# The last of four transposed tiles goes from DMA to TensorE, and a hand-written order is laid out anew

## The chip, the core and the metric

The kernel runs on one core of one Trainium2 chip. The metric is the device time of one execution in microseconds. The kernel before takes 169.82 us, the median of three runs (169.5 to 170.22).

## What is computed

The reference is one pre-norm transformer block on a 2048 x 512 activation in bf16: linear attention with 32 heads of width 16, then a dense layer with relu. Cut to what matters:

```python
x = A_x                                   # 1 x 2048 x 512
n = layernorm(x)                          # over the last axis, eps 1e-5, no gain or bias
q, k, v = heads(n @ wqkv)                 # 32 heads of 16
pq, pk = phi(q), phi(k)                   # phi(t) = where(t > 0, t + 1, exp(t)) + 1e-6
kv = einsum("bhsd,bhse->bhde", pk, v);  z = sum over s of pk
o = einsum("bhqd,bhde->bhqe", pq, kv) / (einsum("bhqd,bhd->bhq", pq, z) + 1e-6)
h = x + o.reshape(B, S, D) @ wo
out = h + relu(layernorm(h) @ w1) @ w2    # w1 512 x 1792, w2 1792 x 512
```

## The kernel before

Every instruction's place is written by hand. `ORDER` (line 18) is a string of words such as `x.2` or `p.0.11.7`; the loop at the end (line 564) takes them one by one and calls `op_x(2)`, `op_p(0, 11, 7)` and so on. Each engine, and each engine's DMA queue, works through its own instructions in the order of the words. The numbers in a word are the tile or block, the piece, and for words of TensorE the PSUM bank (of eight) that takes the result. An operation waits until its inputs are there and until the bank or buffer that it writes has been read.

The 2048 rows are 16 tiles of 128, and four blocks of four tiles. The work runs through these stages:

- First norm: `lx` loads x on SP's queue, `S` and `A` take statistics on VectorE (lines 254, 255), `R` makes the reciprocal deviation on ScalarE (260, 261), `N` normalises on VectorE (268). The normalised tile is transposed into `lnT` either by TensorE (`T`, line 293, four 128 x 128 transposes against the identity) with a copy out of PSUM by ScalarE (`E`, line 303), or by a DMA transpose on SP's queue (`X`, line 314).
- Keys and state: `K` (322) are the key projections, `F`, `U`, `M`, `D` (340, 343, 347, 350) apply phi, `G` (374) collects the state. `za` to `zh` add up the keys, `z` (398) reduces them on TensorE.
- Queries: `Q` (330) projects, `qF`, `qU`, `qM`, `qD` apply phi, again at lines 340 to 350. `d4` (446), `dl4` and `dx4` (452, 457) make one over the denominator of a block. `wb` (474) writes it to a scratch in DRAM, and eight `rb` or `ab` (477) read it back, spread over the partitions, into `rr`. `dm` (493) multiplies the queries of a block with `rr`, in two halves; it needs all eight loads.
- `kv`, `kx`, `m`, `mA`, `mD` (420 to 438) join the state with `wv` and `wo` into one 512 x 512 matrix.
- `h` (502) multiplies and `hD` (508) adds x: tile t of the attention's result.
- Second norm: `s` and `a` (256, 257) take the statistics of h, `n` on VectorE (276) or `nA` on ScalarE (282) subtracts the mean into `hn`; `x` (315) transposes `hn` into `lnT` by DMA on SP's queue. All 16 tiles go this way, `x.0` to `x.3` for block 0. The deviation is applied at the very end.
- First FFN matmul: `p` (517) makes one of 14 pieces of a block from `w1` and all four tiles of `lnT`. For four pieces of block 0 it is split: `ph` (526) takes two tiles at a time, half 0 (tiles 0 and 1) and half 1 (tiles 2 and 3). `pD` on VectorE (537), once `pA` on ScalarE (532), applies relu to two pieces at once.
- Second FFN matmul: `f` (546) multiplies with `w2`, 14 matmuls a tile, mostly in two groups of seven. `fo` (554) scales and adds h, `fd` (561) stores. The last tile is cut by columns.

The words that the change adds use two functions that stand in the kernel and that the old order does not call:

```python
def op_t(t, b):
    at_bank["t", t, 0] = transpose(hn[:, t % NQ, :], b, 0, KD)

def op_v(t):
    nc.vector.tensor_copy(out=lnT_of(t), in_=at_bank["t", t, 0])

op_x = lambda t: nc.sync.dma_start_transpose(out=lnT_of(t), in_=hn[:, t % NQ, :])
```

`transpose` (line 290) issues four 128 x 128 transposes into one bank as bf16; the copy moves 128 x 512 bf16 from that bank to `lnT`.

Of the kernel before, what the change touches and what calls it, by code (L numbers as in the profile page):

```python
# [15 lines left out]


ORDER = """
table const lx.0.1 warm.66.7.64 lx.1.1 masks lx.2.1 lk.0.4 lx.3.1 S.0 lx.4.2 S.1 lx.6.2 lq.0.4 A.0 A.1 S.2 R.0.1
warm.2.7 lx.8.4 R.1.1 N.0 lx.12.4 A.2 N.1 T.0.1 R.2.1 T.1.5 E.0 N.2 E.1 T.2.2 S.3 K.0.0 E.2 A.3 S.4 K.2.2.2.2  # L20
R.3.1 K.2.2.0.2 F.0.1 N.3 S.5 U.0.1 T.3.3 K.1.6.0.2 E.3 A.4 A.5 K.1.6.2.2 S.7 R.4.2 K.3.1.0.2 M.0.1 F.1.1 S.6
K.3.1.2.2 U.1.1 Q.0.1.5 N.4 F.2.1 A.6 N.5 A.7 F.3.1 T.4.6 M.1.1 X.5 D.0.1 Q.0.0.4 R.6.2 D.1.1 M.2.1 U.3.1 M.3.1
Q.0.2.0 N.7 lo.0.2 E.4 S.9 X.7 U.2.1 Q.0.3.1 N.6 qU.0.0.2 D.3.1 K.4.2 S.15 X.6 qF.0.0.2 S.8 K.5.3 D.2.1 qM.0.0.2
qF.0.2.2 G.3 A.8 A.9 S.12 R.8.2 G.0 S.14 F.4.2 N.9 G.2 A.12 N.8 X.9 U.4.2 S.13 G.1 A.15 A.14 A.13 qD.0.0.2 X.8
R.12.2 K.6.2 qU.0.2.2 M.4.2 S.11 K.7.3 lv.0.2 R.14.2 N.12 N.13 X.12 K.9.1 S.10 F.6.2 D.4.2 K.8.0 U.6.2 lv.2.2 A.10
M.6.2 X.13 G.4 N.14 U.8.2 N.15 D.6.2 G.5 X.15 F.8.2 za.4.1 G.6 A.11 X.14 M.8.2 K.12.0 R.10.2 qM.0.2.2 N.10 K.13.1
N.11 X.10 D.8.2 G.7 za.6.0 F.12.2 X.11 K.14.2 U.12.2 qD.0.2.2 K.15.3 M.12.2 l1.2.2 za.8.0 l2.0.7 K.10.0 F.14.2
D.12.2 K.11.1 U.14.2 zf G.9 M.14.2 F.10.2 D.14.2 G.8 U.10.2 zhi M.10.2 G.12 zlo D.10.2 G.14 z.1.0 z.2.0 z.3.0
z.0.0 G.15 zc zh d4.0.3 G.11 dl4.0 dx4.0 G.10 wb.0 G.13 lo.2.2 Q.1.0.1 gA.2.2 gD.0.2 rb.0.6 Q.1.1.2 ab.0.3 rb.0.2
ab.0.7 rb.0.4 kv.0.0 kv.2.0 ab.0.1 rb.0.0 kv.1.0 kv.3.0 ab.0.5 l1.0.2 Q.1.3.6 kx qF.1.0.2 Q.1.2.5 qU.1.0.2  # L30
qM.1.0.2 m.0.3 m.1.4 Q.2.3.7 qF.1.2.2 mD.0.2 Q.2.1.1 qU.1.2.2 qM.1.2.2 dm.0.0.2 m.2.3 m.3.4 Q.2.0.0 dm.0.2.2
mA.2.2 qD.1.0.2 h.1.6 qU.2.0.2 qD.1.2.2 h.0.2 hD.1 qF.2.0.2 h.3.3 s.1 hD.0 Q.2.2.6 a.1 s.0 nA.1 d4.1.2 a.0 h.2.1
hD.3 x.1 nA.0 s.3 qF.2.2.2 Q.3.0.5 x.0 a.3 hD.2 dl4.1 Q.3.3.4 n.3 qU.2.2.2 s.2 x.3 Q.3.2.3 a.2 dx4.1 n.2 Q.3.1.6
qM.2.0.2 qF.3.2.2 x.2 qM.2.2.2 ph.0.2.0.0 qU.3.2.2 qM.3.2.2 ph.0.3.1.0 wb.1 ph.0.0.2.0 qF.3.0.2 qD.3.2.2
ph.0.1.3.0 qD.2.2.2 ph.0.1.3.1 qU.3.0.2 ph.0.0.2.1 qM.3.0.2 rb.1.6 p.0.11.7 rb.1.3 pD.0.0.2 rb.1.1 ph.0.3.1.1
rb.1.0 p.0.10.6 qD.2.0.2 rb.1.7 qD.3.0.2 rb.1.4 p.0.9.2 rb.1.2 pD.0.10.2 rb.1.5 p.0.6.5 l2.7.7 d4.2.6.2 ph.0.2.0.1
dl4.2 p.0.5.4 r.0.4 dm.1.0.2 dl4.3 p.0.4.3 dx4.2 dm.1.2.2 h.4.7 pD.0.2.2 wb.2 pA.0.4.2 p.0.7.6 dx4.3 hD.4 p.0.8.1
pD.0.6.2 h.5.7 pD.0.8.2 rb.2.4 p.0.13.4 rb.2.7 rb.2.3 hD.5 h.6.5 rb.2.0 rb.2.6 f.1.2.0.7 hD.6 rb.2.5 s.5 rb.2.2
rb.2.1 p.0.12.3 wb.3 h.7.1 pD.0.12.2 f.0.7.7.7 hD.7 s.4 f.2.4.0.7 s.7 a.5 a.4 dm.2.0.2 f.1.2.7.7 n.4 dm.2.2.2 a.7
n.5 rb.3.2 s.6 rb.3.6 h.9.0 rb.3.3 h.8.1 x.4 hD.9 a.6 f.0.7.0.7 n.7 r.4.4 fo.1 x.7 n.6 s.9 f.3.5.0.7 rb.3.1 x.6  # L40
h.10.0 x.5 h.11.3 f.3.5.7.7 f.2.4.7.7 fo.3 hD.8 fd.3 rb.3.7 p.1.13.2 fo.2 rb.3.4 fd.1 hD.11 p.1.12.1 rb.3.5 a.9
fo.0 fd.2 p.1.2.6 rb.3.0 hD.10 p.1.3.7 pD.1.12.2 p.1.6.0 pD.1.2.2 p.1.0.3 dm.3.0.2 p.1.7.1 dm.3.2.2 h.13.7
pD.1.6.2 p.1.1.4 hD.13 p.1.4.5 pD.1.0.2 p.1.5.6 s.13 p.1.9.3 pD.1.4.2 h.12.7 p.1.8.2 hD.12 s.10 p.1.11.5 s.8
p.1.10.4 pD.1.8.2 h.14.1 s.11 h.15.7 hD.14 a.10 f.7.0.0.7 a.11 n.9 hD.15 n.11 pD.1.10.2 f.6.7.0.7 a.8 n.10 r.8.4
s.14 x.10 f.4.1.0.7 n.8 x.8 f.5.5.0.7 x.9 f.5.5.7.7 x.11 f.4.1.7.7 fo.5 fd.0 s.12 a.13 f.7.0.7.7 a.12 fo.4 a.14
f.6.7.7.7 fo.7 n.14 n.12 s.15 p.2.10.5 fo.6 p.2.11.6 n.13 fd.6 a.15 n.15 r.12.4 x.12 p.2.13.1 p.2.12.0 fd.5 x.13
p.2.9.4 pD.2.12.2 p.2.8.3 x.15 p.2.2.1 pD.2.8.2 x.14 p.2.3.2 pD.2.10.2 p.2.0.3 fd.7 pD.2.2.2 p.2.1.4 p.2.7.6
pD.2.0.2 p.2.6.5 p.3.8.1 pD.2.6.2 p.3.9.2 p.3.12.3 pD.3.8.2 p.3.13.4 p.3.2.0 pD.3.12.2 p.2.4.6 p.3.10.5 p.3.6.1
p.2.5.7 p.3.4.3 pD.2.4.2 p.3.5.4 p.3.7.2 f.11.7.0.7 pD.3.6.2 pD.3.4.2 f.11.7.7.7 p.3.3.1 f.10.3.7.7 pD.3.2.2
p.3.11.6 p.3.0.4 pD.3.10.2 f.8.1.0.7 f.10.3.0.7 p.3.1.5 f.8.1.7.7 pD.3.0.2 fo.10 f.15.0.0.14.3.1 f.15.6.0.14.0.2  # L50
fo.15.3.1 fd.15.3.1 f.13.4.0.7 fo.15.0.2 fd.15.0.2 fd.4 f.13.4.7.7 f.14.5.7.7 fo.13 fo.11 fd.13 fd.10 f.12.6.0.7
fo.8 fd.8 fd.11 f.14.5.0.7 f.9.7.0.7 f.9.7.7.7 f.12.6.7.7 fo.9 fo.14 fd.9 f.15.3.0.14.2.1 fd.14 fo.12 fd.12
fo.15.2.1 fd.15.2.1
"""


# [540 lines left out]
```

## Time and profile before

| | |
|---|---|
| median of three runs | 169.82 us (169.5 to 170.22) |
| the profiled execution's own time | 169.75 us |
| its span, first to last instruction | 168.0 us |
| granted TensorE clock | 0.999 |
| DMA moved | 16.28 MB, mean 97 GB/s |
| HBM read, written | 9.96 MB, 2.62 MB |

The profile is one execution. PE is TensorE's matmuls, PEld its weight loads, DVE is VectorE, ACT is ScalarE, SP and ACT with a q are their DMA queues. L517 is line 517 of the kernel. A row of a timeline has the start, the length, the engine, the line and what is written from what; `[0.60 <-DMA lnT<-hn]` says how long the engine sat idle before it and what ended that. Matmuls overlap by 0.16 us: one of 512 columns lasts 0.379 us and the next begins 0.216 after it.

### The profile page before, as it was taken

The page shows a single profiled execution, that of the slowest core. Times are in us where ns is not written, and L with a number is a line of the kernel's source. Part 1 is how long each engine was busy: PE and PEld are TensorE (multiplying, and loading weights), DVE is VectorE, ACT ScalarE, POOL GpSimd, SP SyncE. Part 2 cuts the span into 40 slices and gives each one's busy share as a digit, 9 for nine tenths or more (in the row PEclk, how much of TensorE's full clock was granted, in tenths as well). Part 3 has the DMA queues.
Part 4 walks back from the last instruction along what each step waited for, and adds up shares of the span by engine and source line. Part 5 has one row for each costly group of instructions (what it writes and reads, how often), then busy time and mean ns, then how long its engine had stood idle before and what let it go on. Part 6 is the DMA issues. An engine that isn't in the chain of part 4 may idle for free.

```text
span 168.0 us, 2376 instructions
## 1 busy us (share of the span) xinstructions
PE 161.2 (96%) x896; PEld 78.3 (47%) x912; DVE 114.3 (68%) x215; ACT 49.4 (29%) x83; POOL 4.8 (3%) x21
## 2 busy tenths in 40 slices
...
GB/s 112 328 313 156 58 182 105 234 238 96 205 138 35 119 92 248 98 105 7 109 71 153 5 4 0 31 102 23 125 94 4 0 0 0 0 0 59 125 0 101
DMA packets 26091, 16.28 MB, mean 97 GB/s; under 512 B 16096, under 2 KB 25056, under 8 KB 26080
## 3 DMA queue, kind: packets, MB, share of 16 engines
...
q8 instruction: 7, 0.11, 0.3%
q14 instruction: 4, 0.03, 0.1%
HBM read 9.96 MB, written 2.62 MB: 75 GB/s over the span
## 4 chain that ended last, share of the span: by engine, by line
PE 84%; DVE 6%; DMA 4%; issue 1%; ACT 1%; SPq 1%; DVEq 0%
PE bk L546 29%; PE bk L517 27%; PE bk L374 8%; PE bk L322 7%; PE bk L502 6%; PE bk L330 4%; DMA x_nat<-in_A_x_dram 2%; DVE h_nat L508 2%; DMA lnT<-hn 1%; PE bk L526 1%; DVE st L256 1%; DVE st L254 1%; SPq L220 1%; DVE pqT L350 1%; PE bk L398 1%
## 5 line engine op out<-in xcount | busy, mean ns | idle before, releaser
L546 PE MATMUL bk<-w_sb,at 128*128 128x512 bf16 (+2 forms) x245 | 49.4, 355 | 0.4
L517 PE MATMUL bk<-lnT,w_sb 128*128 128x512 bf16 x205 | 46.7, 379 | 0.1
L537 DVE TENSOR_SCALAR at<-bk 128x1024 bf16<-128x1024 f32 x27 | 32.5, 1219 | 16.2 <-PE bk L517 15.0
L546 PEld LDWEIGHTS <-at 128*128 128x128 bf16 x252 | 23.5, 98 | 25.2 <-DVE at L537 0.3
L517 PEld LDWEIGHTS <-w_sb 128*128 128x128 bf16 x208 | 20.4, 98 | 23.9
L554 DVE SCALAR_TENSOR_TENSOR gT<-bk,rstd,h_nat 128x512 bf16<-128x512 f32 (+2 forms) x18 | 12.1, 685 | 19.3 <-PE bk L546 13.9
L260 ACT ACTIVATE rstd<-mv,eps 128x2 f32<-128x2 f32 (+2 forms) x14 | 4.1, 293 | 51.7 <-DVE mv L257 48.9
L340 ACT ACTIVATE eb<-bk 128x1024 bf16<-128x1024 f32 (+1 forms) x18 | 16.6, 931 | 4.4 <-PE bk L322 2.6
L343 ACT ACTIVATE rb<-bk 128x1024 bf16<-128x1024 f32 (+1 forms) x18 | 16.5, 930 | 0.0
L502 PE MATMUL bk<-m_sb,pqs 128*128 128x512 bf16 x64 | 15.6, 379 | 0.0
L330 PE MATMUL bk<-lnT,wq_sb 128*128 128x512 bf16 x61 | 15.0, 379 | 0.2
L322 PE MATMUL bk<-wk_sb,lnT 128*128 128x512 bf16 x64 | 14.8, 379 | 0.0
L374 PE MATMUL bk<-at,h_nat 128*128 128x512 bf16 x54 | 13.0, 379 | 0.1
L508 DVE TENSOR_TENSOR h_nat<-bk,x_nat 128x512 bf16<-128x512 f32 x16 | 10.9, 681 | 1.7 <-PE bk L502 1.7
L254 DVE BATCH_NORM_STATS2 st<-x_nat 128x6 f32<-128x512 bf16 x16 | 10.6, 677 | 2.0 <-DMA x_nat<-in_A_x_dram 2.0
L256 DVE BATCH_NORM_STATS2 st<-h_nat 128x6 f32<-128x512 bf16 x16 | 10.8, 685 | 0.1
L502 PEld LDWEIGHTS <-pqs 128*128 128x128 bf16 x64 | 6.2, 98 | 7.6 <-DVE pqs L493 0.5
L374 PEld LDWEIGHTS <-h_nat 128*128 128x128 bf16 x64 | 6.1, 98 | 7.3 <-issue 0.2
L330 PEld LDWEIGHTS <-wq_sb 128*128 128x128 bf16 x64 | 6.2, 98 | 7.1
L322 PEld LDWEIGHTS <-lnT 128*128 128x128 bf16 x64 | 5.9, 98 | 7.5 <-DMA lnT<-h_nat 0.7
L347 DVE TENSOR_SCALAR eb<-eb 128x1024 bf16<-128x1024 bf16 (+1 forms) x18 | 6.7, 386 | 0.7 <-ACT eb L340 0.7
L493 DVE TENSOR_TENSOR pqs<-pqT,rr 128x1024 bf16<-128x1024 bf16 x8 | 5.2, 680 | 1.9 <-DMA rr<-scr 1.9
...
## 6 DMA issues: line engine op xcount, KB each, us to landing
w_sb<-in_B_w_dram SPq DMA_DIRECT2D x4, 896.0 KB, 5.0
...
rr<-scr SPq DMA_DIRECT2D x28, 64.0 KB, 2.6
...
x_nat<-in_A_x_dram SPq DMA_DIRECT2D x2, 256.0 KB, 4.7
...
```

Source lines behind the costliest of these rows:

```text
L254: op_S = lambda t: nc.vector.bn_stats(out=st[:, t, :], in_=x_nat[:, t, :])
L256: op_s = lambda t: nc.vector.bn_stats(out=st2[:, t, :], in_=h_nat[:, t, :])
L322: nc.tensor.matmul(bk[:, b, :], lhsT=lnT[c][:, kd, j * P : (j + 1) * P], rhs=wk_sb[:, kd, :], **part(("k", t), KD),)
L330: nc.tensor.matmul(bk[:, b, :], lhsT=wq_sb[:, kd, j * P : (j + 1) * P], rhs=lnT[c][:, kd, :], start=(kd == 0), stop=(kd == KD - 1),)
L340: nc.scalar.activation(out=buf(eb, kind, i, n), in_=bank(at_bank[kind, i], n), func=ACT.Exp)
L343: nc.scalar.activation(out=buf(rb, kind, i, n), in_=bank(at_bank[kind, i], n), func=ACT.Relu)
L374: nc.tensor.matmul(bk[:, KD + kd, :], lhsT=ln_nat[:, t, kd * P : (kd + 1) * P], rhs=pk(t)[:, 0, :], start=(not stated), stop=(len(stated) ...
L502: nc.tensor.matmul(bk[:, b, :], lhsT=pqs[:, (c * KD + jb) % NQ, j * P : (j + 1) * P], rhs=m_sb[:, jb, :], start=(jb == 0), stop=(jb == KD ...
L508: nc.vector.tensor_tensor(out=h_nat[:, t : t + n, :], in0=bank(at_bank["h", t], n), in1=x_nat[:, t : t + n, :], op=ALU.add,)
L517: nc.tensor.matmul(bk[:, b, :], lhsT=w1_sb[:, kd, f * P : (f + 1) * P], rhs=lnT[c][:, kd, :], start=(kd == 0), stop=(kd == KD - 1),)
L537: nc.vector.tensor_scalar(out=acts[c % 2][:, f : f + n, :], in0=bank(at_bank["p", c, f], n), scalar1=-1.0, scalar2=0.0, op0=ALU.mult, op1= ...
L546: nc.tensor.matmul(bk[:, b, 0 : w * P], lhsT=acts[c % 2][:, f, j * P : (j + 1) * P], rhs=w2_sb[:, f, k * P : (k + w) * P], **part(("f", t, ...
```

## The change

Nothing but `ORDER` differs; it is one text line shorter, so each function stands one line higher (L525 after is L526 before). The words are the same but for one: `x.2` is gone, and `t.2.2` and `v.2` have come. Tile 2, the last tile of block 0, is now transposed by TensorE into bank 2 and copied to `lnT` by VectorE; tiles 0, 1 and 3 go by DMA as before. The words stand in another order in nearly every line, and TensorE's results are spread over the banks differently.

The parts that the text speaks of; first the first norm's transposes (`X`), the loads (`lv`, `lo`, `l1`, `l2`) and the key projections (`K`):

```diff
-R.12.2 K.6.2 qU.0.2.2 M.4.2 S.11 K.7.3 lv.0.2 R.14.2 N.12 N.13 X.12 K.9.1 S.10 F.6.2 D.4.2 K.8.0 U.6.2 lv.2.2 A.10
-M.6.2 X.13 G.4 N.14 U.8.2 N.15 D.6.2 G.5 X.15 F.8.2 za.4.1 G.6 A.11 X.14 M.8.2 K.12.0 R.10.2 qM.0.2.2 N.10 K.13.1
-N.11 X.10 D.8.2 G.7 za.6.0 F.12.2 X.11 K.14.2 U.12.2 qD.0.2.2 K.15.3 M.12.2 l1.2.2 za.8.0 l2.0.7 K.10.0 F.14.2
...
+F.3.1 lo.2.2 D.0.1 Q.0.2.0 E.4 X.6 M.2.1 M.3.1 qF.0.0.2 S.9 K.4.2 S.13 qU.0.0.2 X.7 K.5.3 A.9 D.2.1 A.8 S.12 R.8.2
+G.2 lv.2.2 F.4.2 A.13 D.3.1 N.8 G.0 qM.0.0.2 X.8 U.4.2 S.15 G.1 M.4.2 qU.0.2.2 N.9 K.6.2 A.12 S.14 X.9 R.12.2 G.3
...
+G.4 S.10 X.14 F.8.2 A.11 G.5 D.6.2 U.8.2 A.10 X.15 za.4.1 K.13.2 R.10.2 K.12.1 N.11 N.10 X.11 qM.0.2.2 G.6 U.12.2
+M.8.2 za.6.0 K.15.3 X.10 F.12.2 G.7 D.8.2 l2.0.7 M.12.2 K.14.2 qD.0.2.2 l1.2.2 lv.0.2 za.8.0 K.11.1 U.14.2 K.10.0
```

The second norm of block 0, the halves of its first FFN matmuls, and `rr` of block 1 (`wb.1`, `rb.1`) with the `w2` weights (`l2.7.7`):

```diff
-mA.2.2 qD.1.0.2 h.1.6 qU.2.0.2 qD.1.2.2 h.0.2 hD.1 qF.2.0.2 h.3.3 s.1 hD.0 Q.2.2.6 a.1 s.0 nA.1 d4.1.2 a.0 h.2.1
-hD.3 x.1 nA.0 s.3 qF.2.2.2 Q.3.0.5 x.0 a.3 hD.2 dl4.1 Q.3.3.4 n.3 qU.2.2.2 s.2 x.3 Q.3.2.3 a.2 dx4.1 n.2 Q.3.1.6
-qM.2.0.2 qF.3.2.2 x.2 qM.2.2.2 ph.0.2.0.0 qU.3.2.2 qM.3.2.2 ph.0.3.1.0 wb.1 ph.0.0.2.0 qF.3.0.2 qD.3.2.2
-ph.0.1.3.0 qD.2.2.2 ph.0.1.3.1 qU.3.0.2 ph.0.0.2.1 qM.3.0.2 rb.1.6 p.0.11.7 rb.1.3 pD.0.0.2 rb.1.1 ph.0.3.1.1
-rb.1.0 p.0.10.6 qD.2.0.2 rb.1.7 qD.3.0.2 rb.1.4 p.0.9.2 rb.1.2 pD.0.10.2 rb.1.5 p.0.6.5 l2.7.7 d4.2.6.2 ph.0.2.0.1
-dl4.2 p.0.5.4 r.0.4 dm.1.0.2 dl4.3 p.0.4.3 dx4.2 dm.1.2.2 h.4.7 pD.0.2.2 wb.2 pA.0.4.2 p.0.7.6 dx4.3 hD.4 p.0.8.1
...
+h.1.6 qM.1.2.2 qD.1.2.2 qU.2.0.2 h.3.7 hD.1 h.0.3 s.1 d4.1.2 a.1 hD.3 nA.1 Q.3.3.1 hD.0 dl4.1 x.1 Q.3.2.0 s.0
+h.2.3 a.0 s.3 nA.0 a.3 qU.3.2.2 Q.3.0.6 x.0 n.3 hD.2 Q.2.3.5 qF.3.2.2 s.2 x.3 Q.3.1.7 dx4.1 a.2 n.2 qM.2.0.2
+qF.2.2.2 t.2.2 wb.1 ph.0.2.0.0 v.2 l2.7.7 ph.0.1.3.0 qU.3.0.2 qM.2.2.2 ph.0.0.2.0 qD.2.0.2 ph.0.2.0.1 qU.2.2.2
+qM.3.2.2 rb.1.6 ph.0.0.2.1 qD.3.2.2 rb.1.1 ph.0.3.1.1 qF.3.0.2 rb.1.0 qD.2.2.2 ph.0.1.3.1 rb.1.7 p.0.6.5 r.0.4
+qM.3.0.2 rb.1.4 pD.0.0.2 p.0.7.6 rb.1.2 rb.1.3 ph.0.3.1.0 pD.0.6.2 p.0.5.4 p.0.4.3 qD.3.0.2 rb.1.5 pD.0.2.2
+d4.2.6.2 p.0.8.5 dl4.2 pA.0.4.2 p.0.9.6 dx4.2 dm.1.2.2 p.0.13.2 dl4.3 wb.2 dm.1.0.2 p.0.11.3 dx4.3 p.0.12.1 rb.2.4
```

Behind them, `rr` of blocks 2 and 3, `h` of block 2 and the transposes of block 1:

```diff
-pD.0.6.2 h.5.7 pD.0.8.2 rb.2.4 p.0.13.4 rb.2.7 rb.2.3 hD.5 h.6.5 rb.2.0 rb.2.6 f.1.2.0.7 hD.6 rb.2.5 s.5 rb.2.2
-rb.2.1 p.0.12.3 wb.3 h.7.1 pD.0.12.2 f.0.7.7.7 hD.7 s.4 f.2.4.0.7 s.7 a.5 a.4 dm.2.0.2 f.1.2.7.7 n.4 dm.2.2.2 a.7
-n.5 rb.3.2 s.6 rb.3.6 h.9.0 rb.3.3 h.8.1 x.4 hD.9 a.6 f.0.7.0.7 n.7 r.4.4 fo.1 x.7 n.6 s.9 f.3.5.0.7 rb.3.1 x.6
-h.10.0 x.5 h.11.3 f.3.5.7.7 f.2.4.7.7 fo.3 hD.8 fd.3 rb.3.7 p.1.13.2 fo.2 rb.3.4 fd.1 hD.11 p.1.12.1 rb.3.5 a.9
...
+f.2.4.0.7 pD.0.12.2 rb.2.5 rb.2.0 rb.2.3 pD.0.8.2 p.0.10.2 wb.3 rb.2.2 h.5.0 rb.2.7 pD.0.10.2 rb.2.6 h.6.1 rb.2.1
+hD.5 h.4.3 hD.6 h.7.2 s.6 f.1.0.0.7 hD.7 hD.4 dm.2.0.2 f.1.0.7.7 dm.2.2.2 s.7 rb.3.4 h.8.1 rb.3.1 s.4 rb.3.5 a.7
+f.0.7.7.7 a.6 a.4 rb.3.3 n.4 hD.8 rb.3.7 n.6 rb.3.6 s.5 h.10.5 x.6 a.5 fo.1 r.4.4 f.0.7.0.7 rb.3.2 hD.10 x.4 n.5
+s.10 f.2.4.7.7 fo.0 n.7 s.8 x.7 h.11.7 f.3.0.7.7 hD.11 fd.0 x.5 f.3.0.0.7 rb.3.0 h.9.1 fo.3 p.1.11.3 s.11 fo.2
```

And the places late in the kernel where seven `w2` matmuls stand between a pair of FFN results and the next use of one of their banks:

```diff
-p.3.11.6 p.3.0.4 pD.3.10.2 f.8.1.0.7 f.10.3.0.7 p.3.1.5 f.8.1.7.7 pD.3.0.2 fo.10 f.15.0.0.14.3.1 f.15.6.0.14.0.2
...
+f.7.4.7.7 n.15 fo.5 s.13 f.7.4.0.7 n.12 n.14 x.12 a.13 n.13 r.12.4 p.2.6.6 fo.7 x.15 f.6.5.0.7 pD.2.6.2 x.14
+p.2.9.7 fd.5 f.6.5.7.7 x.13 p.2.8.6 fd.7 fo.6 p.2.10.2 pD.2.8.2 p.2.3.5 pD.2.10.2 p.2.0.6 p.2.1.7 p.3.6.3 pD.2.0.2
...
+p.3.10.0 p.3.4.1 p.3.8.6 pD.3.4.2 p.2.12.3 pD.3.8.2 p.2.13.4 p.3.1.2 pD.2.12.2 p.3.0.1 f.8.3.7.7 pD.3.0.2 p.3.11.1
```

More of the change, by code (lines that the diff above doesn't have):

```diff
@@ L18 @@
 ORDER = """
[L19 to L23, printed above, removed]
@@ L24 @@
-qF.0.2.2 G.3 A.8 A.9 S.12 R.8.2 G.0 S.14 F.4.2 N.9 G.2 A.12 N.8 X.9 U.4.2 S.13 G.1 A.15 A.14 A.13 qD.0.0.2 X.8
-R.12.2 K.6.2 qU.0.2.2 M.4.2 S.11 K.7.3 lv.0.2 R.14.2 N.12 N.13 X.12 K.9.1 S.10 F.6.2 D.4.2 K.8.0 U.6.2 lv.2.2 A.10
-M.6.2 X.13 G.4 N.14 U.8.2 N.15 D.6.2 G.5 X.15 F.8.2 za.4.1 G.6 A.11 X.14 M.8.2 K.12.0 R.10.2 qM.0.2.2 N.10 K.13.1
-N.11 X.10 D.8.2 G.7 za.6.0 F.12.2 X.11 K.14.2 U.12.2 qD.0.2.2 K.15.3 M.12.2 l1.2.2 za.8.0 l2.0.7 K.10.0 F.14.2
-D.12.2 K.11.1 U.14.2 zf G.9 M.14.2 F.10.2 D.14.2 G.8 U.10.2 zhi M.10.2 G.12 zlo D.10.2 G.14 z.1.0 z.2.0 z.3.0
```

31 lines of the change are left out of this document (17 added, 14 removed).

## The prediction

> **What bounds the kernel now.** I read the page's shares of busy time first, then busy time by stretches, then the timeline where TensorE idles.
>
> ```profile
> span 168.0 us, 2376 instructions
> PE 161.2 (96%) x896; PEld 78.3 (47%) x912; DVE 114.3 (68%) x215; ACT 49.4 (29%) x83; POOL 4.8 (3%) x21
> ...
> 12.00:56.00 44.00, 43.71 (x251) 20.34 (x254) 36.22 (x81) 32.48 (x47) 0.00 (x0) 1.00 0.53 142
> 56.00:60.00 4.00, 3.40 (x28) 2.64 (x28) 2.49 (x6) 3.19 (x4) 0.00 (x0) 1.00 0.43 98
> 60.00:147.00 87.00, 86.49 (x406) 39.59 (x413) 59.47 (x90) 5.22 (x13) 0.00 (x0) 1.00 0.22 61
> 147.00:168.00 21.00, 17.74 (x109) 9.44 (x109) 7.30 (x11) 0.00 (x0) 0.00 (x0) 1.00 0.17 57
> ```
>
> The columns of the stretches are: stretch and length, busy time of PE, PEld, DVE, ACT, POOL (instructions in brackets), granted clock, DMA share, GB/s. TensorE is full, and its clock is granted whole (1.00) in every stretch. Between 12 and 147 us only the stretch 56 to 60 loses more than half a per cent of its length; the rest of the idle time is the start and the tail after the last matmul, which the change leaves alone. So nothing that only relieves another engine counts. What counts is TensorE work added, and when its inputs come. The change sits on the one real hole:
>
> ```profile
> 52.59 3.62 PE L330 MATMUL bk<-lnT,wq_sb 128*128 128x512 bf16 x15
> 55.62 0.10 PEld L330 LDWEIGHTS <-wq_sb 128*128 128x128 bf16 x1
> 56.06 1.77 PEld L526 LDWEIGHTS <-w_sb 128*128 128x128 bf16 x17 [0.35 <-issue]
> 56.09 1.92 PE L526 MATMUL bk<-lnT,w_sb 128*128 128x256 bf16 x16
> 58.62 1.03 PE L526 MATMUL bk<-lnT,w_sb 128*128 128x256 bf16 x8 [0.60 <-DMA lnT<-hn]
> ...
> 51.04 1.58 ACT L282 ACTIVATE hn<-h_nat,mv 128x512 bf16<-128x512 bf16 x2 [1.00 <-DVE mv L257]
> 51.78 5.57 SPq L315 DMA_TRANSPOSE lnT<-hn  x4
> ...
> 54.83 2.52 SPq L315 DMA_TRANSPOSE lnT<-hn  x2
> ...
> 55.09 0.35 DVE L276 TENSOR_SCALAR hn<-h_nat,mv 128x512 bf16<-128x512 bf16 x1
> ...
> 56.14 2.43 DMA lnT<-hn
> ```
>
> The last projection matmul (L330) ends at 56.21 and was due to be followed at 56.05 (56.21 − 0.38 + 0.216, the spacing of 512-column matmuls: (3.62 − 0.38)/15). Sixteen half-wide L526 are 0.110 apart ((1.92 − 0.27)/15), so the seventeenth was due at 57.85. It began at 58.62, when the fourth transpose (x.2, issued 56.14, landed 58.57) was there: **0.77 us lost**, and 0.04 to 0.08 more at 56.06, where the weight load waited for x.0. Together about 0.85. The normalised tile itself was ready at 55.44: the loss is the transfer and its place behind three others on SP's queue (four issues in 5.57 us).
>
> **The change part by part.** (1) *The DMA x.2 goes.* TensorE gets the 0.85 back if nothing replaces it: −0.85. SP is free 1.2 us sooner, which moves wb.1 and what follows it forward.
>
> (2) *Four transposes and a copy come.* Their prices:
>
> ```profile
> 8.71 0.40 PE L293 MATMUL bk<-ident,h_nat 128*128 128x128 bf16 x4
> 9.14 0.60 ACT L303 ACTIVATE lnT<-bk 128x512 bf16<-128x512 bf16 x1
> ...
> L508 DVE TENSOR_TENSOR h_nat<-bk,x_nat 128x512 bf16<-128x512 f32 x16 | 10.9, 681 | 1.7 <-PE bk L502 1.7
> L389 DVE CAST zhl<-zacc 128x512 bf16<-128x512 f32 x1 | 0.4, 417 | 0.0
> ```
>
> Four transposes occupy TensorE 0.23 us (the next matmul after the four at 8.71 starts at 8.94): **+0.22**. The copy out by VectorE (v.2, bf16 from PSUM) is in no row. Bounds: 0.42, its copy of 512 floats from SBUF, to 0.69, its 512-element work on floats in PSUM. I take 0.5, nearer the copy. The bank of t.2 is asked for again by the third half-wide group: t.2 ends at 56.27, its result shows 0.16 later at 56.43, v.2 ends between 56.9 and 57.2; TensorE gets there at 57.14 (56.27 + 8 × 0.110): 0 to 0.05, taken as 0. VectorE itself is held 0.5 longer, ahead of block 1's eb, pqT and the first FFN copy; it idles 1.93 us before dm.1 (row in (6)), which takes that up. Were that gone, the FFN copies and the banks they free would come 0.5 later. The Trainium skill, "VectorE: DVE Perf Modes", section "The TRN2 errata", gives 120 + elements/acceleration cycles at 0.96 GHz out of PSUM, by estimate 0.39 us at twice the rate and 0.66 us at once; by either figure the sum would not move, and no row here decides between them.
>
> (3) *n.2 now has to be on time.* t.2 waits for n.2 (55.44 before), due on TensorE at 56.05. VectorE does the same set of operations up to n.2, but three or four more of them directly follow the one they depend on. In the VectorE timeline a dependent neighbour starts after the end (h_nat ends 49.60, its statistics start 49.63), an independent one before it (statistics end 50.32, next h_nat starts 50.24):
>
> ```profile
> 48.91 0.69 DVE L508 TENSOR_TENSOR h_nat<-bk,x_nat 128x512 bf16<-128x512 f32 x1
> 49.63 0.69 DVE L256 BATCH_NORM_STATS2 st<-h_nat 128x6 f32<-128x512 bf16 x1
> 50.24 0.67 DVE L508 TENSOR_TENSOR h_nat<-bk,x_nat 128x512 bf16<-128x512 f32 x1
> ```
>
> That is 0.11 each, so n.2 ends near 55.9, and its weight load would have gone at 55.84. Cost 0 to 0.2: **+0.1**. The three remaining transposes keep their order x.1, x.0, x.3; tile 0's statistics now stand behind another tile's addition (0.68), which the wait for x.1's long issue nearly covers. x.3 still lands near 57.3 (issued at 54.83, the last but one of the four, 2.43 to its landing as for x.2); TensorE reaches the first half that needs it at 57.6 (56.27 + 12 × 0.110). Cover 0.3.
>
> (4) *Banks handed round anew.* Where two FFN results are copied together and a bank of theirs is asked for again seven 512-column matmuls later, there is a short wait:
>
> ```profile
> 147.78 1.39 PEld L546 LDWEIGHTS <-at 128*128 128x128 bf16 x7
> 148.19 1.23 DVE L537 TENSOR_SCALAR at<-bk 128x1024 bf16<-128x1024 f32 x1 [3.52 <-PE bk L517]
> 149.47 0.52 PEld L546 LDWEIGHTS <-at 128*128 128x128 bf16 x9 [0.30 <-DVE at L537]
> ```
>
> The load was due at 149.29 (147.78 + 7 × 0.216) and ran at 149.47: 0.18 late, of which the matmul lost some 0.05, as loads run one matmul ahead. The old order has one such place; the new one three (p.0.12, p.2.6 and p.3.0, each with seven w2 matmuls behind it). Two more at 0.05 to 0.18: **+0.1**.
>
> (5) *The first norm's transfers.* Two weight loads wait for transposed tiles:
>
> ```profile
> 28.20 2.27 PEld L322 LDWEIGHTS <-lnT 128*128 128x128 bf16 x12 [0.38 <-DMA lnT<-h_nat]
> 30.82 0.55 PEld L322 LDWEIGHTS <-lnT 128*128 128x128 bf16 x4 [0.34 <-DMA lnT<-h_nat]
> ...
> 29.61 1.08 SPq L226 DMA_DIRECT2D w_sb<-in_B_w_dram  x2
> ...
> 41.55 1.09 PEld L420 LDWEIGHTS <-wv_sb 128*128 128x128 bf16 x16
> ...
> wv_sb<-in_A_wqkv_dram SPq DMA_DIRECT2D x2, 256.0 KB, 3.1
> ```
>
> The brackets are the loads' lateness; as in (4) the matmuls lose about a third of it, 0.1 to 0.2 for both. The new order takes both wv_sb loads out from where they stood among the last six transposes, and moves K.13 ahead of eight matmuls (1.7 us) that stood before it. From −0.2 (both waits go) to +0.2 (K.13 waits longer than these): **−0.05**. One wv_sb load now stands behind both large weight loads, issued near 31 (29.61 + 1.08, and its own turn). With 3.1 us for itself and 5.0 for the weights ahead (row in (6)) it is there by 39; TensorE wants it at 41.55. Cover 2.5, cost 0.
>
> (6) *The w2 weights (l2.7.7) go ahead of rr's eight loads of block 1* on SP, where they came after.
>
> ```profile
> w_sb<-in_B_w_dram SPq DMA_DIRECT2D x4, 896.0 KB, 5.0
> rr<-scr SPq DMA_DIRECT2D x28, 64.0 KB, 2.6
> ...
> 65.18 1.29 DVE L493 TENSOR_TENSOR pqs<-pqT,rr 128x1024 bf16<-128x1024 bf16 x2 [1.93 <-DMA rr<-scr]
> ```
>
> Issued near 57, the weights land near 62; the program makes the eighth rr load wait for that, so it lands near 62 + 2.6 = 64.6, and VectorE had waited to 65.18 before. Behind that dm.1 stand pD.0.12 and pD.0.8 on VectorE, and pD.0.12 waits for a later matmul anyway. Cost 0, and 1:1 with whatever rr lands later than about 67. The Trainium skill speaks against this edit: "DMA: Bandwidth & Descriptors", section "Queues, rings and completion order", says that each DMA engine takes descriptors in ring order, so the small loads would stand behind 896 KB. By it they could not start before 62, which is the bound just worked out.
>
> **Sum:** −0.85 + 0.22 + 0.1 + 0.1 − 0.05 = −0.48 on the profiled execution's 169.75 (168.0 of span and 1.75 around it): 169.27. The median before is 169.82, 0.07 above, so **169.3**.
>
> **The rivals.** *A. Nothing new waits.* n.2 is in time, the banks fit, the loads of (5) go: −0.85 + 0.22 − 0.1, and the one bank wait of before goes too, −0.05 to −0.18: 168.85. For it: VectorE's order is free elsewhere. Against: (3) and (4) have almost no cover.
>
> *B. The wait moves on.* The transposes left in the queue come late instead: x.3 (cover 0.3), or in block 1 x.5, which now has fd.0 and three more rr loads ahead of it on SP. Price 0.3 to 0.6: 169.8.
>
> *C. Slower, by rr of block 2.* One group of seven w2 matmuls now comes after h.8 instead of before, so TensorE asks for dm.2 sooner.
>
> ```profile
> L477 SPq DMA_DIRECT2D rr<-scr x8: 312/418/426, 68.6 to 72.1; - x8
> ...
> DMA to landing us min/median/max: 2.5/2.7/3.3
> 77.10 0.66 DVE L493 TENSOR_TENSOR pqs<-pqT,rr 128x1024 bf16<-128x1024 bf16 x1
> 77.94 0.68 DVE L493 TENSOR_TENSOR pqs<-pqT,rr 128x1024 bf16<-128x1024 bf16 x1
> 78.93 0.53 PEld L502 LDWEIGHTS <-pqs 128*128 128x128 bf16 x3
> ```
>
> h's load came at 78.93; now at 78.93 − 7 × 0.216 + 0.22 − 0.75 (part 1 less part 3) = 76.9. The two dm.2 take 1.34 and a start of 0.1, so rr must be there by 75.4. Its last load was issued at 72.1 and landed by 75.4 at the slowest (3.3), 74.8 at the median. wb.3 now stands among the eight. Every further microsecond goes straight to TensorE: 1.6 late gives 170.9. Against: the chain starts with dx4.2, which has one ScalarE operation ahead of it where three stood, so it should be no later, and with the median landing there is 0.6 to spare.
>
> **How the numbers follow.** Forecast 0.46, A 0.22, B 0.15, C 0.17. A measurement of this kernel tells about 0.5%, 0.85 us, from no change: below 168.97 or above 170.67. Faster: A and 0.03 of the forecast, 0.25. Slower: C but 0.02 of it, with 0.02 from B, 0.17. Within: 0.58. The range reaches from a little under A to C less its upper third: 168.5 to 170.6. The forecast's own is 168.9 to 169.7.
>
> **What would show it.** In the changed profile: L294's four transposes of hn near 56.1 to 56.3 with at most 0.2 idle before them; no idle of L525 for the transfer near 58.6; TensorE's busy time up by about 0.2 and the span down by about 0.5. Short PEld waits for L536 near the three places of (4). Wrong would be: a TensorE wait for lnT in block 0 or 1 (B); a wait of L501 for L492 near 77 us (C); or rr landing after 67 (6).

## The result, and the profile after

Over 20 runs each, taken side by side, the kernel after the change took 169.18 us (168.71 to 170.23) and the kernel before 170.23 us (169.5 to 172.34). The ratio is 0.9949 with a 95% interval of 0.9933 to 0.9965: 0.87 us less, between 0.6 and 1.14. It is worked out from the undisturbed (fast) runs and is not the quotient of the two medians, which lie 1.05 us apart. The prediction said 169.3 us, which by its sum is a ratio of 0.9972 (169.27 of 169.75). Its time is met, in part by luck: the kernel before took 0.41 more here than the 169.82 from which the time was worked out, and that makes up for most of the gain that the forecast left out. Its gain of 0.48 lies just outside the interval on the small side, and what the trace shows is nearer to rival A. The prediction counted less than 0.5% as no change and gave that a chance of 0.58; the 0.51% measured lies on that line.

The page of the profile of the kernel after, its shares of busy time and the chain that ended last, and then the busy time by stretches (same columns as in the prediction):

```profile
span 167.4 us, 2392 instructions
PE 162.4 (97%) x916; PEld 79.1 (47%) x916; DVE 116.2 (69%) x216; ACT 49.3 (29%) x83; POOL 4.8 (3%) x21
PE 93%; DMA 2%; DVE 1%; SPq 1%; issue 0%
```

```profile
54.60:60.50 5.90, 5.90 (x46) 4.17 (x45) 5.38 (x12) 5.25 (x8) 0.00 (x0) 1.00 0.70 187
60.50:147.00 86.50, 86.50 (x420) 39.61 (x419) 60.88 (x91) 4.84 (x11) 0.00 (x0) 1.00 0.21 52
```

TensorE is busy through the whole stretch in which the hole was: 5.90 of 5.90 us, where the kernel before had lost most of a microsecond. The number of weight loads is up by four, 912 to 916: the four transposes. The matmul counts (896 and 916) can't be compared that way, because records are missing from the trace of before; so the account below is made of start times and not of busy time.

The timeline of the kernel after, around the second norm of block 0:

```profile
51.37 4.62 SPq L314 DMA_TRANSPOSE lnT<-hn  x3
54.14 2.11 PE L329 MATMUL bk<-lnT,wq_sb 128*128 128x512 bf16 x9
55.47 0.35 DVE L275 TENSOR_SCALAR hn<-h_nat,mv 128x512 bf16<-128x512 bf16 x1
55.87 0.42 PEld L292 LDWEIGHTS <-hn 128*128 128x128 bf16 x4
56.09 0.39 PE L292 MATMUL bk<-ident,hn 128*128 128x128 bf16 x4
56.31 3.22 PE L525 MATMUL bk<-lnT,w_sb 128*128 128x256 bf16 x28
56.58 0.42 DVE L311 COPY lnT<-bk 128x512 bf16<-128x512 bf16 x1 [0.42 <-PE bk L292]
59.37 1.89 PE L516 MATMUL bk<-lnT,w_sb 128*128 128x512 bf16 x8
```

Three transposes are left in SP's queue. The normalised tile (L275) ends at 55.82. The four transposes begin at 56.09, which is when the last projection matmul hands over (54.14 + 9 × 0.216 = 56.08), and the half-wide matmuls follow at 56.31. Twenty-eight of them run without a break: one is 0.109 long ((3.22 − 0.27)/27), 28 × 0.109 = 3.06, and the next line starts at 59.37 = 56.31 + 3.06.

For the head of the two kernels, weight loads from their timelines; first before, then after. The row starts directly behind the transposes of tile 3 of the first norm, which wait until that tile is normalised.

```profile
8.88 0.58 PEld L322 LDWEIGHTS <-lnT 128*128 128x128 bf16 x4
```

```profile
9.01 0.58 PEld L321 LDWEIGHTS <-lnT 128*128 128x128 bf16 x4
```

And the first FFN rows and the last run of loads of the kernel before, and then the last loads of the kernel after (the last load starts 0.10 before the end of such a row):

```profile
59.49 1.03 PE L517 MATMUL bk<-lnT,w_sb 128*128 128x512 bf16 x4
...
161.96 2.71 PEld L546 LDWEIGHTS <-at 128*128 128x128 bf16 x22
```

```profile
162.05 2.06 PEld L545 LDWEIGHTS <-at 128*128 128x128 bf16 x19
```

From these the half microsecond can be followed from stage to stage:

| stage | before | after | difference |
|---|---|---|---|
| head: load after tile 3's transposes | 8.88 | 9.01 | +0.13 |
| from there to the end of block 0's projections | 47.21 (to 56.09) | 47.08 (to 56.09) | −0.13 |
| the four transposes | none | 0.22 | +0.22 |
| 24 (before) or 28 (after) half-wide matmuls beyond 0.109 each | 3.40 − 2.62 = 0.78 | 0 | −0.78 |
| start of the last weight load | 164.57 | 164.01 | −0.56 |

The first four differences add up to −0.56, so nothing is gained or lost between 60 and 164 us. The span goes down by 0.6 (168.0 to 167.4). The head begins with the same instructions in both kernels and is late by its loads of `x_nat`, a matter of the execution. Without it the kernel gains 0.69, inside the interval of 0.6 to 1.14.

### The profile page after: what moved, and what is told of

It reads as the page before. It is cut to its first block, busy times and chain, and to the rows that moved or that the text cites. A ratio compares the mean times of both kernels' runs of the same rounds, so it can differ in the third digit from the quotient of the medians.

```text
span 167.4 us, 2392 instructions
## 1 busy us (share of the span) xinstructions
PE 162.4 (97%) x916; PEld 79.1 (47%) x916; DVE 116.2 (69%) x216; ACT 49.3 (29%) x83; POOL 4.8 (3%) x21
## 3 DMA queue, kind: packets, MB, share of 16 engines
HBM read 9.96 MB, written 2.62 MB: 75 GB/s over the span
## 4 chain that ended last, share of the span: by engine, by line
PE 93%; DMA 2%; DVE 1%; SPq 1%; issue 0%
PE bk L545 29%; PE bk L516 27%; PE bk L373 8%; PE bk L329 8%; PE bk L501 8%; PE bk L321 7%; DMA x_nat<-in_A_x_dram 2%; PE bk L525 2%; DVE st L253 1%; SPq L219 1%; PE bk L445 1%; PE bk L397 1%; PE bk L419 1%; PE bk L431 1%; PE bk L292 1%; SPq L225 0%
## 5 line engine op out<-in xcount | busy, mean ns | idle before, releaser
L545 PE MATMUL bk<-w_sb,at 128*128 128x512 bf16 (+2 forms) x252 | 50.4, 355 | 0.0
L267 DVE TENSOR_SCALAR h_nat<-x_nat,mv,rstd 128x512 bf16<-128x512 bf16 x16 | 6.1, 405 | 0.3 <-ACT rstd L260 0.3
```

What stands on the lines that cost most here:

```text
L545: nc.tensor.matmul(bk[:, b, 0 : w * P], lhsT=acts[c % 2][:, f, j * P : (j + 1) * P], rhs=w2_sb[:, f, k * P : (k + w) * P], **part(("f", t, ...
```

## The experiments

Theory: the gain is the wait for the fourth transfer (0.85) less the work of four transposes (0.22), and nothing else in the new order reaches TensorE. Rivals: the new order brings the gain itself (R1); the gain is held down by new waits with thin cover, those of (3), (4), (6) and rival C (R2); it is the transfer's place in the queue that counts, so that any one tile fewer on SP would do (R3). Each kernel was run beside the one before, whose median was 169.9 to 170.23 in these runs; so the ratios compare better than the medians. The last three columns are read from the timelines in the way just shown: the head's load after tile 3's transposes, the first matmul behind block 0's projections, and the time from that matmul to the last weight load, in which neither the head nor the first norm has a part.

| kernel | median us | ratio to before (95%) | load after tile 3 | block 0's matmul | from it to the last load |
|---|---|---|---|---|---|
| before | 170.23 | 1 | 8.88 | 56.09 | 108.48 |
| after | 169.18 | 0.9949 (0.9933 to 0.9965) | 9.01 | 56.09 | 107.92 |
| e1_x2_back | 170.07 | 1.0007 (0.9992 to 1.0022) | 8.73 | 56.14 | 108.88 |
| e2_t2_alone | 169.46 | 0.9971 (0.9945 to 0.9998) | 9.36 | 56.60 | 108.23 |
| e3_three_t2 | 169.60 | 0.9976 (0.9957 to 0.9994) | 8.75 | 56.09 | 108.37 |
| e4_l2_behind | 169.12 | 0.9949 (0.9929 to 0.9969) | 8.78 | 55.85 | 107.93 |
| e5_dm2_late | 169.25 | 0.9951 (0.9933 to 0.9969) | 9.08 | 56.15 | 107.92 |
| e6_act_copy | 169.17 | 0.9955 (0.9937 to 0.9973) | 8.94 | 56.01 | 107.99 |
| e7_n2_late | 169.10 | 0.9946 (0.9932 to 0.9961) | 8.95 | 56.04 | 107.93 |
| e8_t3_too | 169.12 | 0.9945 (0.9928 to 0.9961) | 8.96 | 56.03 | 108.15 |
| e9_x4_dma | 170.02 | 1.0004 (0.9981 to 1.0026) | 8.78 | 56.62 | 107.93 |
| e10_t3_not_t2 | 170.08 | 0.9998 (0.9971 to 1.0025) | 10.07 | 57.15 | 108.60 |

**e1_x2_back** puts the DMA back into the new order.

```diff
-qF.2.2.2 t.2.2 wb.1 ph.0.2.0.0 v.2 l2.7.7 ph.0.1.3.0
+qF.2.2.2 x.2 wb.1 ph.0.2.0.0 l2.7.7 ph.0.1.3.0
```

> The changed kernel with tile 2 transposed by DMA again (x.2 behind x.3), all else as changed. Wait theory: the gain is TensorE no longer waiting for that transfer. TensorE would want tile 2 at 57.4, x.2 is issued near 56.05 and lands near 58.5, so it waits 0.9 to 1.1 us and saves 0.22 us of transposes: span 168.1 to 168.3 against 167.4, about the time of before. Order theory (the new order brings the gain, the transposes little): span at most 167.6.

The ratio is 1.0007: the whole gain is gone. The timeline of this kernel, TensorE's part:

```profile
56.14 1.47 PE L525 MATMUL bk<-lnT,w_sb 128*128 128x256 bf16 x12
58.63 1.58 PE L525 MATMUL bk<-lnT,w_sb 128*128 128x256 bf16 x13 [1.01 <-DMA lnT<-hn]
```

The hole is back at the same place, under the name of the DMA. The transfer is there at the same time as before (58.63, where before had 58.62), but in the new order only 12 half-wide matmuls stand ahead of it and not 16, so TensorE is due at 56.14 + 12 × 0.109 = 57.45 and loses 1.18. R1 falls: the new order with the DMA still in it is worth nothing; its interval leaves 0.14 us at most on the good side. (It isn't quite the order alone that is tried, since the hole is 0.4 longer in it than before.)

**e2_t2_alone** is the other half: the kernel before, with t.2 and v.2 in place of x.2.

```diff
-qM.2.0.2 qF.3.2.2 x.2 qM.2.2.2 ph.0.2.0.0 qU.3.2.2
+qM.2.0.2 qF.3.2.2 t.2.2 qM.2.2.2 ph.0.2.0.0 v.2 qU.3.2.2
```

> The kernel before with only x.2 replaced by the four transposes into bank 2 and VectorE's copy; order and banks as before. Wait theory: -0.85 + 0.22, span 167.3 to 167.5, ratio to before near 0.996. Order theory: the transposes cost 0.22 and another wait takes the place of the old one, span 168.0 or more.

The ratio is 0.9971 (0.9945 to 0.9998): a gain, and by its middle a smaller one than that of the whole change, though the intervals overlap. In its timeline the 24 half-wide matmuls take 2.62 again (56.92 to 59.54), so the hole of block 0 is closed. But in block 3 loads wait for `pqs`. The same place, first in before, then in e2:

```profile
95.02 0.19 PEld L502 LDWEIGHTS <-pqs 128*128 128x128 bf16 x2 [0.24 <-DVE pqs L493]
```

```profile
94.01 1.29 DVE L493 TENSOR_TENSOR pqs<-pqT,rr 128x1024 bf16<-128x1024 bf16 x2 [0.18 <-issue]
94.76 0.11 PEld L502 LDWEIGHTS <-pqs 128*128 128x128 bf16 x2 [0.35 <-DVE pqs L493]
...
95.36 0.11 PEld L502 LDWEIGHTS <-pqs 128*128 128x128 bf16 x2 [0.49 <-DVE pqs L493]
```

The load of before waits too, but the four matmuls behind it keep their spacing (1.03 us). In e2, by the steady spacing of the loads, TensorE loses 0.22, and another 0.10 goes where the half-wide matmuls start 0.32 behind t.2 and not 0.22. The last column says the same: 108.23 is 0.25 under before and 0.31 over after. So in this profile less than half of the gain gets through. Why `pqs` is late is not shown. The head of this profile is 0.48 late, so TensorE comes to this place no earlier than in before (its FFN matmuls ahead of it start at 88.69, in before at 88.64); VectorE starts `pqs` 0.32 later (94.01 for 93.69), 0.18 of it idle for no reason that the profile shows. Nor does one profile tell whether every execution loses this: the ratio gives 0.49 us for this kernel and 0.87 for the whole change. In after nothing waits for `pqs` at all.

**e3_three_t2** does t.2 three times over, into the same bank: the same result with eight more matmuls of TensorE's work.

```diff
-qF.2.2.2 t.2.2 wb.1
+qF.2.2.2 t.2.2 t.2.2 t.2.2 wb.1
```

> The changed kernel with the four transposes of tile 2 issued three times over into the same bank (eight more transposes of 128 x 128; the output stays the reference's). If TensorE's work sets the end there and nothing covers it, +0.43 us (8 x 0.054): span 167.8 to 167.9. If the stage has slack that the transposes hide in, no change.

Its row has "x12" in place of "x4" transposes, and the half-wide matmuls start 0.67 behind it (56.09 to 56.76) instead of 0.22. From block 0 to the last load it takes 0.45 longer than in after, and the ratio is 0.0027 higher, 0.46 us. Four transposes cost 0.22, and what TensorE is given to do goes to the end one to one: nothing behind block 0 has slack to swallow it.

**e4_l2_behind** moves the w2 weights behind the eight rr loads again, as they were before.

```diff
-wb.1 ph.0.2.0.0 v.2 l2.7.7 ph.0.1.3.0
+wb.1 ph.0.2.0.0 v.2 ph.0.1.3.0
...
-p.0.4.3 qD.3.0.2 rb.1.5 pD.0.2.2
+p.0.4.3 qD.3.0.2 rb.1.5 l2.7.7 pD.0.2.2
```

> The changed kernel with the 896 KB load of w2 weights (l2.7.7) behind the eight rr loads of block 1 again. Covered theory: rr of block 1 lands near 62.5 to 63 in place of 64.9, VectorE's 0.75 us wait before dm.1 goes, TensorE sees nothing: span 167.3 to 167.5. Rival (the load ahead of rr costs time): span below 167.1.

The ratio is that of the change, 0.9949. The timelines, first of after, then of e4:

```profile
58.08 3.12 SPq L476 DMA_DIRECT2D rr<-scr  x7
65.00 1.29 DVE L492 TENSOR_TENSOR pqs<-pqT,rr 128x1024 bf16<-128x1024 bf16 x2 [0.75 <-DMA rr<-scr]
```

```profile
57.76 3.60 SPq L476 DMA_DIRECT2D rr<-scr  x8
63.93 1.28 DVE L492 TENSOR_TENSOR pqs<-pqT,rr 128x1024 bf16<-128x1024 bf16 x2
```

And from the answers for the tile `rr`, the time of its loads from issue to landing, again after and then e4:

```profile
DMA to landing us min/median/max: 2.2/2.6/4.7
```

```profile
DMA to landing us min/median/max: 2.3/2.6/3.4
```

Behind the weights an rr load takes up to 4.7 us and VectorE waits 0.75 for rr; with rr ahead the longest of the whole kernel is 3.4 (block 1's eight take 2.5 to 2.7), and VectorE's two operations start 1.1 earlier with no wait (0.24 of this only because block 0 begins that much earlier in this profile). TensorE sees neither (107.93 for 107.92). The cover of (6) is shown.

**e5_dm2_late** delays what rival C makes late: a statistics step goes ahead of dm.2 on VectorE.

```diff
-hD.4 dm.2.0.2 f.1.0.7.7 dm.2.2.2 s.7 rb.3.4
+hD.4 s.7 dm.2.0.2 f.1.0.7.7 dm.2.2.2 rb.3.4
```

> The changed kernel with the statistics s.7 ahead of dm.2 on VectorE instead of behind it, so dm.2 ends 0.60 us later. In the changed profile dm.2 ends at 76.74 and h.8's weight load goes at 76.86. If that place has no more cover than those 0.12 us: TensorE waits 0.45 to 0.5 us at h.8 for pqs, span 167.8 to 167.9. If there is cover that the rows do not show: no change. In both cases rr is not what ends the wait (it had landed at 74.4).

The second case: no time is lost. In the timeline of this kernel the two `pqs` start at 76.12, where after has 75.46 (0.06 of the difference is this profile's later block 0):

```profile
76.12 1.27 DVE L492 TENSOR_TENSOR pqs<-pqT,rr 128x1024 bf16<-128x1024 bf16 x2
76.92 0.31 PEld L501 LDWEIGHTS <-pqs 128*128 128x128 bf16 x2
77.14 1.03 PE L501 MATMUL bk<-m_sb,pqs 128*128 128x512 bf16 x4
...
77.45 0.22 PEld L501 LDWEIGHTS <-pqs 128*128 128x128 bf16 x2 [0.21 <-DVE pqs L492]
```

The second of them ends at 77.39. The third load, which needs it, comes at 77.45 and not at 77.35, and is shown as waiting. Yet the four matmuls take 1.03 = 0.38 + 3 × 0.216: they follow each other without a gap. Two things give this cover. Half the loads need only the first result, and a weight load runs one matmul (0.216) ahead of its own.

**e6_act_copy** lets ScalarE do the copy.

```diff
-wb.1 ph.0.2.0.0 v.2 l2.7.7
+wb.1 ph.0.2.0.0 e.2 l2.7.7
```

> The changed kernel with tile 2 copied out of PSUM by ScalarE (as the first norm's tiles are) and not by VectorE. ScalarE is through with its exponential at 56.7, so the copy ends near 57.2, before the bank (57.3) and the tile (57.6) are asked for; its queue then runs 0.5 later, with 0.3 to 0.5 of cover at the next banks. If the engine of the copy does not matter: span 167.3 to 167.6. If ScalarE's queue is tight: TensorE waits for banks near 59 to 62 us, span 167.7 or more.

0.9955 against 0.9949: no difference. ScalarE's copy takes 0.61 where VectorE's takes 0.42, and the way from block 0 to the last load is 0.07 longer. Which engine copies doesn't matter here.

**e7_n2_late** puts the last tile's normalisation (n.2) behind one more operation on VectorE.

```diff
-a.2 n.2 qM.2.0.2 qF.2.2.2
+a.2 qM.2.0.2 n.2 qF.2.2.2
```

> The changed kernel with n.2 behind one 0.42 us operation of VectorE (qM.2.0), so that the tile is normalised 0.34 us later. If n.2 is on TensorE's path without cover: 0.15 to 0.35 us of idle time before the four transposes, span 167.55 to 167.75. If it has cover: no change.

No time is lost here either. The rows of its timeline:

```profile
54.29 1.89 PE L329 MATMUL bk<-lnT,wq_sb 128*128 128x512 bf16 x8
55.63 0.35 DVE L275 TENSOR_SCALAR hn<-h_nat,mv 128x512 bf16<-128x512 bf16 x1
56.03 0.23 PEld L292 LDWEIGHTS <-hn 128*128 128x128 bf16 x4 [0.34 <-DVE hn L275]
56.04 0.40 PE L292 MATMUL bk<-ident,hn 128*128 128x128 bf16 x4
```

The tile ends at 55.98, 0.16 later than in after (0.34 was expected), and the load waits for it by name. The matmul was due at 54.29 + 8 × 0.216 = 56.02 and starts at 56.04. A wait of 0.34 in the load's bracket, and 0.02 lost. How much later than this the tile might come wasn't tried; the load already starts as late as its matmul allows. With e5 this is against R2: neither of the two thinnest covers holds the gain down.

**e8_t3_too** gives tile 3 to TensorE as well.

```diff
-s.2 x.3 Q.3.1.7 dx4.1 a.2 n.2 qM.2.0.2 qF.2.2.2 t.2.2 wb.1 ph.0.2.0.0 v.2
+s.2 Q.3.1.7 dx4.1 a.2 n.2 qM.2.0.2 qF.2.2.2 t.3.1 t.2.2 wb.1 ph.0.2.0.0 v.3 v.2
```

> The changed kernel with tile 3 transposed by TensorE and copied by VectorE as well; x.3 goes. Wait theory: no wait for x.3 is left to remove, so only the work counts, +0.22, span 167.6 to 167.7. Rival (each DMA transpose less helps): span below 167.3.

From block 0 to the last load it takes 0.23 more than in after. So x.3 was in time, and taking it out of the queue is work for nothing. The total, 0.9945, doesn't show this: in this profile the time from the last load to the end of the span is 167.4 − 164.18 = 3.2, where after has 167.4 − 164.01 = 3.4. The median over four runs can't tell 0.2 us from nothing, so the cost stands for TensorE alone.

**e9_x4_dma** goes the other way in the first norm: its tile 4, done by TensorE before and after, goes by DMA.

```diff
-N.4 Q.0.1.7 N.5 F.2.1 D.1.1 X.5 U.2.1 N.6 T.4.3 N.7 U.3.1 Q.0.3.1 S.8
+N.4 X.4 Q.0.1.7 N.5 F.2.1 D.1.1 X.5 U.2.1 N.6 N.7 U.3.1 Q.0.3.1 S.8
...
-Q.0.2.0 E.4 X.6 M.2.1
+Q.0.2.0 X.6 M.2.1
```

> The changed kernel with the opposite exchange in the first norm: tile 4 goes by DMA (x.4 of the first norm, ahead of the other DMA transposes) and not by TensorE and ScalarE. Wait theory: what counts is whether the tile arrives before TensorE asks. Tile 4 is normalised at 11.75, would land near 14.3, and is asked for at 14.3; the transposes behind it move by up to 0.4 with 0.5 us and more of cover. Then 0.22 us of TensorE's work goes: span less head 0.2 lower, total 168.9. If it lands late, up to 0.4 of wait takes the gain.

The hope was to save 0.22; the ratio is 1.0004, so the whole gain of the change is spent. Weight loads in its timeline:

```profile
14.16 0.55 PEld L321 LDWEIGHTS <-lnT 128*128 128x128 bf16 x4 [0.48 <-DMA lnT<-h_nat]
15.45 0.55 PEld L321 LDWEIGHTS <-lnT 128*128 128x128 bf16 x4 [0.73 <-DMA lnT<-h_nat]
...
21.90 0.55 PEld L321 LDWEIGHTS <-lnT 128*128 128x128 bf16 x4 [0.73 <-DMA lnT<-h_nat]
22.60 0.49 PEld L321 LDWEIGHTS <-lnT 128*128 128x128 bf16 x3 [0.15 <-DMA lnT<-h_nat]
```

The first norm now has twelve transfers and not eleven. The one more pushes the others back in SP's queue, and TensorE waits for it and for three more places behind it: the cover of 0.5 and more that was expected there is gone. From the head's load to block 0 it takes 47.84 (8.78 to 56.62) and not 47.08: 0.76 more, with 0.22 of work taken out, so 0.98 of waiting; behind block 0 it runs as after does (107.93).

**e10_t3_not_t2** tests R3: tile 3 by TensorE, tile 2 by DMA. SP's queue has as many transposes as in the changed kernel, but the tile that is ready last is the one that goes by DMA.

```diff
-s.2 x.3 Q.3.1.7 dx4.1 a.2 n.2 qM.2.0.2 qF.2.2.2 t.2.2 wb.1 ph.0.2.0.0 v.2
+s.2 Q.3.1.7 dx4.1 a.2 n.2 qM.2.0.2 qF.2.2.2 x.2 t.3.2 wb.1 ph.0.2.0.0 v.3
```

> The changed kernel with tile 3 on TensorE and tile 2, the one normalised last, by DMA. It tells the place in SP's queue from the transfer: x.2 has no other transpose ahead of it any more, is issued at 55.9 and lands at 58.3, wanted at 57.5. If the transfer itself is what is late: TensorE waits 0.7 to 0.9 us, span 168.1 to 168.3. If it was the place behind three others: the wait is under 0.3, span below 167.8.

The ratio is 0.9998. The timeline, VectorE's normalisation of tile 2 and TensorE's part, and then the transfer as it stands in the chain that ended last:

```profile
56.54 0.35 DVE L275 TENSOR_SCALAR hn<-h_nat,mv 128x512 bf16<-128x512 bf16 x1
...
57.15 0.39 PE L292 MATMUL bk<-ident,hn 128*128 128x128 bf16 x4
57.37 1.47 PE L525 MATMUL bk<-lnT,w_sb 128*128 128x256 bf16 x12
59.36 0.81 PE L525 MATMUL bk<-lnT,w_sb 128*128 128x256 bf16 x6 [0.52 <-DMA lnT<-hn]
```

```profile
56.92 2.40 DMA lnT<-hn
```

TensorE was due at 57.37 + 12 × 0.109 = 58.68: 0.68 lost, and the last column has the same 0.68 over after. R3 falls for this order. The transfer is issued at 56.92, 0.03 after its tile is ready (56.89), so its place in the queue costs nothing and the 0.68 is the transfer alone: 2.40, where there are 1.79 from the normalisation to the use (56.89 to 58.68). The old order leaves more room, 2.41 (ready at 55.44, due at 57.85), and there x.2 went 0.70 late, at 56.14, behind x.3. By estimate from these rows it would have landed at 57.87 if sent at once. So any one transfer fewer might have closed most of the hole in the old order; that was not run. (This profile is also some 1.06 late from its head on, which the last section takes up; the 0.68 doesn't contain that.)

None of the ten beats the changed kernel beyond the noise.

## Why the prediction was right, and where it was not

One reading ahead of the sum is off: the stretches 12 to 56 and 60 to 147 also lose more than half a per cent, 0.66 and 0.59 (43.71 of 44.00 and 86.49 of 87.00). Matmul records are missing there (251 and 406, for 254 and 413 loads), and the sum doesn't use it.

**(1) The DMA goes: −0.85.** Right; measured are 0.78 in the hole and 0.04 at x.0, together −0.82. The hole is closed in after (28 matmuls in 3.06), and e1 and e10 bring it back with the DMA, at 1.18 and 0.68. The prediction laid the loss to "the transfer and its place behind three others". In the old order the place was 0.70 of the delay (ready at 55.44, issued at 56.14); in the new order, which asks for the tile 1.79 after it is ready and not 2.41, the transfer alone is too long (e10).

**(2) Four transposes +0.22, copy 0.5.** The transposes are right to the hundredth (56.09 to 56.31), and e3 shows the term by adding it twice more (0.45). The copy took 0.42, at the lower bound; the value taken, 0.5, was too high and cost nothing. The Trainium skill, "VectorE: DVE Perf Modes", section "The TRN2 errata", gave by estimate 0.39 at twice the rate and 0.66 at once: the measured 0.42 goes with the faster.

**(3) n.2 in time: +0.1.** The time was right (end at 55.82 for an estimated 55.9), its price was not: 0. The range of 0 to 0.2 took the load's due time as TensorE's. e7 makes the tile 0.16 later still and TensorE loses 0.02. x.3, with a cover of 0.3, was in time; e8 shows that it had nothing to give.

**(4) Banks: +0.1.** Wrong in its mechanism. The row at 149.47 of before is a load that reads `at`, which VectorE had just written: a wait for data. It was read as a wait for a bank. At the places named after has no such wait, because a bank is asked for by the matmul, one spacing later, and not by the load. The rows of after, first around p.0.10 (behind p.0.12), then around p.3.11 (behind p.3.0):

```profile
68.01 1.39 PEld L545 LDWEIGHTS <-at 128*128 128x128 bf16 x7
68.43 3.67 DVE L536 TENSOR_SCALAR at<-bk 128x1024 bf16<-128x1024 f32 x3 [2.13 <-PE bk L516]
69.52 0.74 PEld L516 LDWEIGHTS <-w_sb 128*128 128x128 bf16 x4
...
140.73 1.23 DVE L536 TENSOR_SCALAR at<-bk 128x1024 bf16<-128x1024 f32 x1 [0.50 <-PE bk L516]
141.83 0.74 PEld L516 LDWEIGHTS <-w_sb 128*128 128x128 bf16 x4
142.04 1.03 PE L516 MATMUL bk<-lnT,w_sb 128*128 128x512 bf16 x4
```

The loads run on the beat (68.01 + 7 × 0.216 = 69.52). The copy that begins at 140.73 ends at 141.96, after the load at 141.83 and before the matmul at 142.04: the load needs no bank, and the matmul finds it free by 0.08. p.2.9, behind p.2.6, has the same cover (load 118.30, end of the copy 118.43, matmul 118.51). The term is 0.

**(5) The first norm's transfers: −0.05.** The stretch got 0.13 shorter, of which some 0.04 is the wait for x.0 that (1) has counted. The waits view of after has no line of TensorE for a transposed tile by DMA, where before had two loads late. That after comes to this stretch 0.13 later than before is not the reason: by the table, new-order profiles that come to it at 8.78 (e4) and at 8.94 to 8.96 (e6, e7, e8), on both sides of before's 8.88, take 47.07 to 47.09 as after does. The gain is not certain in every execution: in e3, with the earlier head of 8.75, one such wait of 0.59 is back and the stretch takes 47.34. For the old order only before tells it, since e2 waits there for another load too, as e1 does. So the theory's "nothing else" is right but for some 0.09 here.

**(6) Weights ahead of rr: 0.** Right. Estimated were 62 for the weights and 64.6 for the last rr load; VectorE's operation got its rr at 65.00, its next FFN copy still waits 2.13 for TensorE at 68.43, and e4 gives the same time with the old place. The Trainium skill, "DMA: Bandwidth & Descriptors", section "Queues, rings and completion order", had small loads stand behind the large one in ring order. The trace agrees: block 1's rr loads take up to 4.7 us behind the weights and 2.5 to 2.7 ahead of them (e4).

**The rivals.** A, "nothing new waits", is what the trace shows: (3) and (4) cost nothing. Its 168.85 is 0.90 less than the profiled execution, and the ratio says 0.87. But that is the low end of its own sum (168.84 to 168.97), which also took 0.05 to 0.18 for a bank wait that isn't one; so it is right in its condition and not in each term. The likeliest case, with +0.2 for (3) and (4), was too cautious by about that much: measured −0.82 + 0.22 − 0.09 = −0.69, forecast −0.48. B fell: x.3 and x.5 were in time. C's estimate of place was exact (h.8's load at 76.86 for 76.9). Nothing was late there in after:

```profile
75.46 1.28 DVE L492 TENSOR_TENSOR pqs<-pqT,rr 128x1024 bf16<-128x1024 bf16 x2
76.86 0.75 PEld L501 LDWEIGHTS <-pqs 128*128 128x128 bf16 x4
```

Its bound, rr there by 75.4, left out both covers that e5 shows: there the same operations came 0.60 later, counted from block 0, at no cost. An rr 1.6 later, its price of 170.9, was not tried.

What stays open: the trace's 0.69 against 0.87 by the ratio and 1.05 between the medians. The interval (0.6 to 1.14) holds all three. Open, too, are the late `pqs` in e2 and how the old order would have done with one transfer fewer.
